# One multiply per turn, half-query waits and a third bank in a four-layer attention kernel with its own planner

## The chip, the cores and the metric

The kernel runs on one core of one Trainium2 chip. The metric is device time in microseconds (us) of one execution. The core has a matrix engine (PE, with its weight load as a row of its own, PEld), a vector engine (DVE), an activation engine (ACT), a general engine (POOL) and a queue engine (SP) that issues nearly all the DMAs here. Matrix results land in PSUM, eight banks of 512 float columns by 128 partitions.

## The reference

The input is a sequence of 2048 rows of width 1024, 32 heads of 32. Four residual layers follow each other, A, B, A, B, with the same weights in both rounds:

```
x = x + A(layernorm(x));  x = x + B(layernorm(x))      # twice
A: q, k, v = x @ wqkv; pq = q @ w_phi; pk = k @ w_phi       # per head
   phi(p) = [softmax(p), softmax(-p)]
   kv = phi(pk)^T v;  z = sum over rows of phi(pk)
   o = (phi(pq) kv) / (phi(pq) z + 1e-6);  A = o @ wo
B: p = softmax(q k^T / sqrt(32));  B = (p v) @ wo           # full attention
```

A is linear in the sequence length. B computes 32 x 2048 x 2048 exponentials in each round, 134 million; they are most of the work of ACT.

## The kernel before, in words

The activations stay transposed in on-chip memory (features on partitions, 2048 rows on the free axis), in four chunks of 512 rows. "Layer" in the code is one round A plus B.

*A.* `layernorm` normalises a chunk; `a_keys` projects keys and values, and adds up kv and z. `a_queries` (line 823) projects a half of the heads of a chunk in four PSUM tiles of class "mm" (class names below), takes two exponentials of each on ACT (line 834), and multiplies by kv (872) and z; `a_out` (898) projects the result in tiles of class "mm" and adds it to x. Each chunk then gets its second layernorm, its keys and values of head group 0 (`b_k`, `b_v`), and chunk 0 its first query (`b_q`).

*B.* Attention goes in turns. A turn is a chunk of 512 queries and a group of four heads: 32 turns a layer, 64 units each. A unit is 128 keys of one head by the 512 queries, one PSUM bank. `group` (1097) takes the next three units, on three different row tiles j of the array, and puts them in one set of three banks: one score group on PE (line 1082), then one exponential on ACT over three banks (1139). Two such sets alternate, so the next score group can be written while ACT works. Some units go to DVE instead (`spare`, `convert`, `exp_dve`): DVE takes a score out of PSUM (1221), and when it has two, computes the exponential by a polynomial (1046, 1048, 1051). When a third unit of a group is lent to DVE, ACT's instruction is two banks wide. A unit may be lent only if everything it needs is done, and DVE looks 36 to 44 units ahead. The exponentials go into the product with v and into the row of ones that gives the denominators (1264); both gather in bank 6.

*A query* has two copies. `b_q` (937) evacuates the projection to copy 0 (DVE, line 943), and `q_swap` writes copy 1 with upper and lower half of the partitions exchanged, by two DMAs (948, 949). Queries of later chunks of the first layers are projected early, sent to DRAM by `q_away` (959) and fetched by `q_back` (three DMAs). A unit with head pair pp and row tile j reads copy (pp + j // 2) mod 2, and of it only the partitions 32j to 32j + 31. `needs` (1076) lists what a unit waits for: the keys, and all three steps of the query.

*End of a turn.* Two half-turns (pp = 0, 1) leave two tiles T, each copied from PSUM by DVE (1279): T[0] has its outputs in partitions 0 to 63 and its denominators in 64 to 127, T[1] the other way round. Four small DMAs (1309) gather the denominators, DVE takes reciprocals (1314), one DMA writes them to DRAM (1315), one reads them back spread over all partitions (1317), and two DVE multiplies of 64 partitions each (1320) make the turn's normalised output oT. The last turn of each layer has a path of its own. The output projection (`b_o`, `b_last`) follows as filler.

*The order.* No line of the code fixes it. Every operation is recorded with an engine, a duration, what it depends on, the buffers it holds and a priority; a planner (`Sched`) runs at build time, starts on each engine the ready operation of the lowest priority number whose buffers can be had, and the instructions are issued in that order. Priorities are times in the planner's units; a turn is 10 of them. `QUOTA` limits the live buffers of a class, among them PSUM classes: "mm" and "fil" had 2. "fil" is the class of filler projections; in attention they have bank 7 alone, before it any bank. Where PE would have nothing to do, the planner puts in matrix passes that compute nothing needed (line 1490 and passes on `onesD`). Engines and the SP queue work strictly in the order issued, PE's weight loads apart. So a change of a quota, of a dependence or of a priority can move any instruction behind it.

Of the kernel before, what the change touches and what calls it, by code (L numbers as in the profile page):

```python
# [10 lines left out]
ACT = mybir.ActivationFunctionType  # L11
ALU = mybir.AluOpType
# [8 lines left out]
C512 = 512  # L21
# [27 lines left out]
class Sched:  # L49
# [133 lines left out]
    def run(self):  # L183
# [27 lines left out]
        while left:  # L211
# [118 lines left out]
EXP2_B, EXP2_C, EXP2_R = -0.9409531310034907, 6.912204565299476, 0.8383392207797716  # L330
LAG = 5
AHEAD_AT = 5
P0 = (133, 163, 246)
# [3 lines left out]
AWAY = (2, 8)  # L337
# [13 lines left out]
def dve_us(n):  # L351
    return n / 960 + 0.15
# [6 lines left out]
def kernel(  # L359
# [11 lines left out]
    nc = tc.nc  # L371
# [85 lines left out]
    op = sch.op  # L457
# [600 lines left out]
    def attention(base, kT, vT, q_of, gate, most, mix, turns, pos):  # L1058
# [17 lines left out]
        def needs(u):  # L1076
            return flat([kT[u[1]][2][u[3] // 2], q_of[(u[0], u[1])][2]])

# [164 lines left out]
        if True:  # L1243
            for qc, g in turns:
# [41 lines left out]
                if end:  # L1286
# [32 lines left out]
                o_b, o_v = sb("oT", C512)  # L1319
                s = [op("DVE", dve_us(512), lambda a=a, k=k, o_v=o_v, r_v=r_v, T=T: nc.vector.tensor_tensor(  # L1320
                    out=o_v()[a, :], in0=T[k][1]()[a, :], in1=r_v()[a, :], op=ALU.mult),
                    [bk], [o_b, r_b, T[k][0]], prio)
                    for k, a in enumerate((lo_, hi_))]
                oTs[qc][g] = (o_b, o_v, s)
# [26 lines left out]
    for layer in range(2):  # L1351
# [18 lines left out]
        for c in chunks:  # L1370
            xnA[c] = layernorm(c, base + 10 * c - 9 if base + c else -16.0, ANY, n=4 if layer else 2)
            a_keys(c, base + 10 * c, wk_s, wv_s, kv, ANY)
# [23 lines left out]
        for c in range(NC):  # L1396
            pr = second + 20 * c
            o_b, o_v = sb("oc", G, C512)
            oc = (o_b, o_v, {})
            for hf in range(2):  # L1400
                a_queries(c, hf, pr + 5 * hf, wq_s, state, oc)
            a_out(c, pr + 22, wo_s, oc)
            xnB[c] = layernorm(c, pr + 23, ANY)
            b_k(0, c, pr + 42, wk0, kT, ANY, "ACT")
            if c == 0:
                q_of[(0, 0)] = b_q(0, 0, pr + 42.5, wq0, ANY)
            for t in range(TB):
                b_v(0, c, t, pr + 43 + 0.1 * t, bv_s[0], vT, ANY, "ACT", (0,) if last else (0, 1))
        gate = []
        at = second + 130  # L1410

        for g in range(1, G):
            pr = at + 10 * pos[(0, g)] - (30 if last else 19)
            w = slab("w2", pr - 1, B_w[:, :, D + g * P:D + (g + 1) * P], P)
            for c in range(NC):
                b_k(g, c, pr + (6 if last else 4) * c, w, kT, FIL, "DVE")
        for c in range(NC):
            for t in range(TB):
                b_v(1, c, t, at + (7 if last else 4.5) * (4 * c + t) + 2, bv_s[1], vT, FIL, "DVE")
                if last:  # L1420
                    b_v(0, c, t, at + 3 * (4 * c + t) + 3, bv_s[0], vT, FIL, "DVE", (1,))
        for g in range(G):
            pr = at + 10 * pos[(0, g)]
            w = slab("w2", pr - 11, B_w[:, :, g * P:(g + 1) * P], P) if g else wq0
            for qc in range(NC):
                if qc < side:
                    if qc or g:
                        pq = at + 10 * pos[(qc, g)]
                        wq = w if pq < pr + 30 else slab("w2", pq - 11, B_w[:, :, g * P:(g + 1) * P], P)
                        q_of[(qc, g)] = b_q(g, qc, pq - 8, wq, FIL)  # L1430
                else:
                    away = q_away(g, qc, pr + (22 if last else AWAY[qc - 2]), w, FIL)
                    q_of[(qc, g)] = q_back(g, qc, at + 10 * pos[(qc, g)] - 12, away)
        oTs = attention(at, kT, vT, q_of, gate, MOST[layer], MIX[layer], turns, pos)
        if last:
            bo_s = [slab("bo", at + 290 + fc, B_o[:, :, fc * C512:(fc + 1) * C512], C512) for fc in range(2)]
        for qc, p0, gap in ((0, P0[0], GAPS[0]), (1, P0[1], GAPS[1]), (2, P0[2], GAPS[2])):
            if last:
                gap = 3.2
                p0 = (226, 252, 278)[qc]  # L1440
# [13 lines left out]
        for i in range(G):  # L1454
            pr = p0 - 7 + 2 * i
            if last:
# [69 lines left out]
```

## Time and profile before

| | us |
|---|---|
| median of 3 runs | 2403.58 (2401.06 to 2406.6) |
| the profiled execution | 2402.28 |
| its span, first to last instruction | 2400.5 |
| PE busy in the span | 2248.0 |
| ACT busy | 2042.4 |
| DVE busy | 1861.2 |
| mean share of the DMA queue of SP | 17.1% of 16 engines |

In the rows that follow, times are from the start of the span. A group row gives line, engine and operation, what it writes and reads, shape, count; then its busy time and the mean of one in ns; then the idle time of the engine ahead of it and what ended it. A mean counts an instruction from its start to its end, and neighbours overlap, so busy times are less than count times mean. Timeline rows give start, length, and in brackets the idle time before. Matrix passes are pipelined and their ends are modelled: a busy PE is not a PE at its peak.

### The profile page before, as it was taken

The numbers are of one execution on the slowest core, as the hardware profiler recorded it, in microseconds if no ns is written. First come the engines' busy times: TensorE is split into PE (matmuls) and PEld (weight loads), VectorE is DVE, ScalarE is ACT, GpSimd is POOL, SyncE is SP. The second block draws the span as 40 slices with busy tenths as digits, with TensorE's granted clock in tenths as the row PEclk, the third lists the DMA queues.
The fourth block names the chain that finished last, engine by engine and source line by source line (L and its number), as shares of the span: only waits on it lengthen the run. The fifth ranks groups of instructions, "written<-read, shape, count | busy, mean of one in ns | idle before, by whom it ended". The sixth has DMA issues, their size and how long they took to land.

```text
span 2400.5 us, 61762 instructions
## 1 busy us (share of the span) xinstructions
PE 2248.0 (94%) x26839; PEld 864.3 (36%) x26904; DVE 1861.2 (78%) x2540; ACT 2042.4 (85%) x1893; POOL 28.0 (1%) x72
## 2 busy tenths in 40 slices
PE   7999999999999998999998999899999999999998
PEld 4443443333333333333333444333333333333333
DVE  6997763565668788987996776456699999998997
ACT  6325657999999999999997456499999999999998
POOL 0000000000000000000000000000000000000000
PEclk9999999999999999999999999899999999999999
DMA  9020010112222221113314100000111111021110
GB/s 220 14 75 1 5 36 17 41 37 48 51 59 73 82 59 55 54 48 110 117 36 143 36 5 25 18 24 26 37 30 41 33 31 33 25 61 42 42 31 28
DMA packets 205192, 117.03 MB, mean 49 GB/s; under 512 B 125304, under 2 KB 194936, under 8 KB 204152
## 3 DMA queue, kind: packets, MB, share of 16 engines
q1 hardware_dynamic: 203864, 110.98, 17.1%
q8 instruction: 210, 3.44, 0.6%
q10 hardware_dynamic: 1056, 2.10, 0.3%
q14 instruction: 62, 0.51, 0.1%
HBM read 77.40 MB, written 15.19 MB: 39 GB/s over the span
## 4 chain that ended last, share of the span: by engine, by line
ACT 35%; PE 13%; issue 9%; DVE 4%; DMA 1%; ACTq 0%; SPq 0%; DVEq 0%
ACT arena L1139 33%; PE psum L503 6%; PE psum L507 2%; PE psum L1082 2%; PE psum L1264 1%; DVE arena L598 1%; ACT arena L696 1%; DVE arena L594 0%; DMA arena<-rd 0%; PE psum L872 0%; DMA arena<-arena 0%; DVE arena L700 0%; PE psum L817 0%; DVE work L1046 0%; DVE arena L709 0%
## 5 line engine op out<-in xcount | busy, mean ns | idle before, releaser
L1139 ACT ACTIVATE arena<-psum 128x1536 bf16<-128x1536 f32 (+1 forms) x1338 | 1712.4, 1553 | 43.0 <-PE psum L1082 38.6
L1264 PE MATMUL psum<-arena 128*32 128x512 bf16 x4096 | 621.1, 383 | 1.5 <-DVE arena L1279 1.4
L1264 PE MATMUL psum<-arena,ones_bf 128*32 128x512 bf16 x4096 | 621.3, 383 | 0.0
L507 PE MATMUL psum<-arena 128*32 128x512 bf16 (+1 forms) x8768 | 607.4, 377 | 12.4 <-DVE xT L1001 2.9
L1082 PE MATMUL psum<-arena 32*128 32x512 bf16 x4096 | 526.5, 383 | 79.2 <-ACT arena L1139 72.7
L503 PE MATMUL psum<-arena 128*128 128x512 bf16 (+1 forms) x1976 | 457.8, 377 | 24.6 <-DVE arena L598 6.0
L1082 PEld LDWEIGHTS <-arena 32*128 32x128 bf16 x4096 | 178.1, 91 | 605.0 <-issue 594.3
L1046 DVE SCALAR_TENSOR_TENSOR work<-work 128x1024 f32<-128x1024 f32 (+1 forms) x310 | 369.4, 1191 | 6.0
L507 PEld LDWEIGHTS <-arena 128*32 128x32 bf16 x8768 | 195.7, 95 | 258.3 <-issue 153.3
L503 PEld LDWEIGHTS <-arena 128*128 128x128 bf16 x2032 | 194.0, 99 | 259.2 <-issue 54.8
L1221 DVE TENSOR_SCALAR work<-psum 128x512 int32<-128x512 f32 x302 | 207.6, 687 | 93.9 <-PE psum L1082 91.2
L1264 PEld LDWEIGHTS <-arena 128*32 128x32 bf16 x4096 | 169.9, 95 | 210.4 <-issue 149.0
L1046 DVE SCALAR_TENSOR_TENSOR arena<-work 128x1024 bf16<-128x1024 f32 (+1 forms) x155 | 184.5, 1190 | 2.6
L1264 PEld LDWEIGHTS <-ones_bf 128*32 128x32 bf16 x4096 | 168.5, 95 | 29.1 <-issue 3.6
L931 DVE CAST arena<-psum 128x512 bf16<-128x512 f32 (+1 forms) x128 | 83.6, 653 | 110.4 <-PE psum L507 110.2
L696 ACT ACTIVATE arena<-psum 128x512 bf16<-128x512 f32 x80 | 42.8, 599 | 85.2 <-PE psum L503 53.8
L1051 DVE TENSOR_SCALAR work<-work 128x1024 int32<-128x1024 int32 (+1 forms) x155 | 104.7, 676 | 3.9
L1048 DVE TENSOR_SCALAR work<-work 128x1024 int32<-128x1024 int32 (+1 forms) x155 | 104.3, 673 | 3.6
L834 ACT ACTIVATE arena<-psum 128x512 bf16<-128x512 f32 x128 | 69.8, 597 | 40.9 <-PE psum L503 32.4
L594 DVE TENSOR_TENSOR arena<-xT,arena 128x1024 f32<-128x1024 bf16 x64 | 78.0, 1220 | 32.3 <-ACT arena L581 32.2
L1279 DVE COPY arena<-psum 128x512 f32<-128x512 f32 x126 | 86.3, 685 | 14.2 <-PE psum L1264 13.2
L507 PE MATMUL psum<-xT,onesD 128*32 128x512 bf16 x1200 | 91.3, 380 | 1.5 <-DVE arena L931 0.6
(97 smaller groups left out, 1387.6 us busy)
## 6 DMA issues: line engine op xcount, KB each, us to landing
arena<-rd SPq DMA_DIRECT2D x62, 256.0 KB
arena<-in_A_wqkv_dram SPq DMA_DIRECT2D x10, 1024.0 KB
arena<-in_B_wqkv_dram SPq DMA_DIRECT2D x35, 256.0 KB
arena<-arena SPq DMA_DIRECT2D x256, 32.0 KB
arena<-in_B_wo_dram SPq DMA_DIRECT2D x32, 256.0 KB
arena<-wd_k SPq DMA_DIRECT2D x8, 1024.0 KB
arena<-arena SPq DMA_DIRECT2D x80, 64.0 KB
arena<-in_A_wo_dram SPq DMA_DIRECT2D x4, 1024.0 KB
```

Source lines behind the costliest of these rows:

```text
L503: nc.tensor.matmul(out_, lhsT=lhsT, rhs=rhs, start=start, stop=stop, skip_group_check=True)
L507: nc.tensor.matmul(out_[ks, :], lhsT=lhsT[:, ks], rhs=rhs, start=start, stop=stop, tile_position=(0, 32 * k), skip_group_check=True)
L594: s1 = op("DVE", dve_us(1024), lambda pr=pr, w_v=w_v: nc.vector.tensor_tensor(out=w_v(), in0=xT[:, pr, csl(c)], in1=m_v().unsqueeze(1).to_ ...
L931: return soon(op("DVE", dve_us(n), lambda: nc.vector.tensor_copy(out=dst(), in_=src()), [dep], bufs, prio))
L1046: return sch.later("DVE", dve_us(n * 512), lambda: nc.vector.scalar_tensor_tensor(out=out_(), in0=in0(), scalar=scalar, in1=in1(), op0=ALU ...
L1048: m = ts(lambda: nc.vector.tensor_scalar(out=x_v().bitcast(I32), in0=y_v().bitcast(I32), scalar1=0x007FFFFF, scalar2=0x3F800000, op0=ALU.b ...
L1051: a = ts(lambda: nc.vector.tensor_scalar(out=y_v().bitcast(I32), in0=y_v().bitcast(I32), scalar1=0x7F800000, scalar2=None, op0=ALU.bitwise ...
L1082: nc.tensor.matmul(out=out_, lhsT=kT[g][1]()[r, pp, d * P:(d + 1) * P], rhs=q_of[(qc, g)][1]()[r, (pp + j // 2) % 2, :], start=True, stop= ...
L1139: ex = make("ACT", act_us(w * C512), lambda: nc.scalar.activation(out=e_v()[:, 0:w * C512], in_=s_v()[:, 0:w * C512], func=ACT.Exp, scale= ...
L1221: pair["got"].append(sch.later("DVE", dve_us(512), lambda: nc.vector.tensor_scalar(out=y_v().bitcast(I32)[:, k, :], in0=s_v(), scalar1=EXP ...
L1264: nc.tensor.matmul(out=a_v()[col:col + 32, :], lhsT=v_v()[:, kc % 4, o:o + DH] if what == 0 else ones_bf[:], rhs=ev()[:, x * C512:(x + 1) ...
L1279: cp = op("DVE", dve_us(512), lambda t_v=t_v, a_v=a_v: nc.vector.tensor_copy(out=t_v(), in_=a_v()), [last], [a_b, t_b], prio - 4)
```

## The change

Four edits, and a set of literals that became names with the values they had.

1. `QUOTA`: "mm" and "fil" from 2 to 3.
2. `needs`: a unit waits only for the step that wrote the partitions it reads: the evacuation for copy 0, one of the two swap DMAs for copy 1.
3. End of a turn: a DMA moves the upper half of T[1] over the upper half of T[0], whose denominators have been read by then; one DVE multiply of 128 partitions makes oT. The move depends on the reciprocals and on the copy of T[1].
4. `QL`: in the second layer the queries are projected at priority 15 ahead of their turn, before 8, and their weight slabs are fetched at 18 ahead, before 11. In the first layer both stay.

```
-QUOTA = {"pk": 3, "pv": 2, "kv": 1, "ln": 2, "mm": 2, "cmp": 2, "bc": 4, "num": 1, "wt": 4, "fil": 2,
+QUOTA = {"pk": 3, "pv": 2, "kv": 1, "ln": 2, "mm": 3, "cmp": 2, "bc": 4, "num": 1, "wt": 4, "fil": 3,
...
+QL = (8, 15)
...
         def needs(u):
-            return flat([kT[u[1]][2][u[3] // 2], q_of[(u[0], u[1])][2]])
+            qc, g, pp, d, j = u
+            q = q_of[(qc, g)][2]
+            return flat([kT[g][2][d // 2], q[(1 if j > 1 else 2) if (pp + j // 2) % 2 else 0]])
...
                 o_b, o_v = sb("oT", C512)
-                s = [op("DVE", dve_us(512), lambda a=a, k=k, o_v=o_v, r_v=r_v, T=T: nc.vector.tensor_tensor(
-                    out=o_v()[a, :], in0=T[k][1]()[a, :], in1=r_v()[a, :], op=ALU.mult),
-                    [bk], [o_b, r_b, T[k][0]], prio)
-                    for k, a in enumerate((lo_, hi_))]
+                mv = dma(prio, lambda T=T: nc.sync.dma_start(out=T[0][1]()[hi_, :], in_=T[1][1]()[hi_, :]),
+                         [rc, T[1][2]], [T[0][0], T[1][0]], kb=128)
+                s = [op("DVE", dve_us(512), lambda o_v=o_v, r_v=r_v, T=T: nc.vector.tensor_tensor(
+                    out=o_v(), in0=T[0][1](), in1=r_v(), op=ALU.mult),
+                    [bk, mv], [o_b, r_b, T[0][0]], prio)]
...
-            w = slab("w2", pr - 11, B_w[:, :, g * P:(g + 1) * P], P) if g else wq0
+            w = slab("w2", pr - (QL[layer] + 3), B_w[:, :, g * P:(g + 1) * P], P) if g else wq0
...
-                        wq = w if pq < pr + 30 else slab("w2", pq - 11, B_w[:, :, g * P:(g + 1) * P], P)
-                        q_of[(qc, g)] = b_q(g, qc, pq - 8, wq, FIL)
+                        wq = w if pq < pr + 30 else slab("w2", pq - (QL[layer] + 3), B_w[:, :, g * P:(g + 1) * P], P)
+                        q_of[(qc, g)] = b_q(g, qc, pq - QL[layer], wq, FIL)
...
```

More of the change, by code (lines that the diff above doesn't have):

```diff
@@ L331 @@
 LAG = 5
+KL = (19, 30)
+KS = (4, 6)
+VS = (4.5, 7)
+VH = 3
+QL = (8, 15)
+AW = 22
+OUT_AT = (226, 252, 278)
+GO = 3.2
+BO = 290
+PT = 2
+QB = 12
+PH = (5, 22, 42)
+LA = 9
 AHEAD_AT = 5
@@ L1370 @@
         for c in chunks:
-            xnA[c] = layernorm(c, base + 10 * c - 9 if base + c else -16.0, ANY, n=4 if layer else 2)
+            xnA[c] = layernorm(c, base + 10 * c - LA if base + c else -16.0, ANY, n=4 if layer else 2)
             a_keys(c, base + 10 * c, wk_s, wv_s, kv, ANY)
@@ L1400 @@
             for hf in range(2):
[L1401 to L1404, printed above, removed]
+                a_queries(c, hf, pr + PH[0] * hf, wq_s, state, oc)
+            a_out(c, pr + PH[1], wo_s, oc)
+            xnB[c] = layernorm(c, pr + PH[1] + 1, ANY)
+            b_k(0, c, pr + PH[2], wk0, kT, ANY, "ACT")
             if c == 0:
-                q_of[(0, 0)] = b_q(0, 0, pr + 42.5, wq0, ANY)
+                q_of[(0, 0)] = b_q(0, 0, pr + PH[2] + 0.5, wq0, ANY)
             for t in range(TB):
-                b_v(0, c, t, pr + 43 + 0.1 * t, bv_s[0], vT, ANY, "ACT", (0,) if last else (0, 1))
+                b_v(0, c, t, pr + PH[2] + 1 + 0.1 * t, bv_s[0], vT, ANY, "ACT", (0,) if last else (0, 1))
         gate = []
@@ L1454 @@
         for i in range(G):
-            pr = p0 - 7 + 2 * i
+            pr = p0 - 7 + PT * i
             if last:
```

17 lines of the change are left out of this document (8 added, 9 removed).

## The prediction

> **What bounds the kernel now.** I read the span by stages first, then the activation engine's groups, then its idle times one by one, then the vector engine and the DMA queue around them. The stages are my cuts: up to 200 us the first layer's key side, to 390 its query side, to 1300 its attention (with the second layer's first keys inside), to 1558 the second layer's linear part, to 2389 its attention, and a tail.
>
> ```profile
> 0.00:200.00 200.00, 176.03 (x1097) 91.27 (x1118) 171.11 (x280) 85.75 (x133) 12.85 (x39) 0.99 0.39 93
> 200.00:390.00 190.00, 181.74 (x991) 74.89 (x1007) 120.18 (x167) 107.82 (x166) 0.00 (x0) 1.00 0.06 15
> 390.00:1300.00 910.00, 855.61 (x11842) 305.88 (x11844) 683.03 (x919) 883.26 (x723) 12.55 (x25) 0.99 0.23 64
> 1300.00:1558.00 258.00, 239.29 (x1359) 106.17 (x1376) 171.95 (x250) 134.32 (x216) 2.59 (x8) 0.97 0.10 33
> 1558.00:2389.00 831.00, 788.76 (x11510) 283.47 (x11507) 708.41 (x915) 829.88 (x654) 0.00 (x0) 1.00 0.12 34
> 2389.00:2400.50 11.50, 6.61 (x63) 2.62 (x57) 6.53 (x10) 1.33 (x3) 0.00 (x0) 1.00 0.27 91
> ```
>
> Columns are stretch, length, then busy time of PE, weight load, DVE, ACT and POOL, granted clock, DMA share and GB/s. In the second attention ACT works 829.88 of 831 us: what leaves ACT there leaves the time. In the first it works 883.26 of 910, so 26.7 us are stalls. The two linear parts are TensorE's. The times of the activation engine that carry the sum:
>
> ```profile
> L1139 ACT ACTIVATE arena<-psum 128x1536 bf16<-128x1536 f32 x1119 | 1569.1, 1621 | 40.2 <-PE psum L1082 36.7 <-PE psum L1264 3.0 <-DVE arena L931 0.4
> L1139 ACT ACTIVATE arena<-psum 128x1024 bf16<-128x1024 f32 x218 | 262.9, 1206 | 2.8 <-PE psum L1082 1.9 <-PE psum L1264 0.9
> L1139 ACT ACTIVATE arena<-psum 128x1536 bf16<-128x1536 f32 x540 | 760.8, 1655 | 2.3 <-PE psum L1082 1.9 <-DVE arena L931 0.4
> L1139 ACT ACTIVATE arena<-psum 128x1024 bf16<-128x1024 f32 x113 | 140.4, 1243 | 0.0
> ```
>
> The first two rows are the whole run, the last two the second attention. One 512-column block more costs 1621 - 1206 = 415 ns in the one, 1655 - 1243 = 412 ns in the other. The 654 instructions of the second attention (540 of three blocks, 113 of two, one of one) filled 829.88 us; with 0.412 per block that leaves about 0.105 us for an instruction itself, so three blocks go through every 1.34 us.
>
> **Part 1: blocks that leave ACT.** The planner decides at build time which blocks of scores DVE exponentiates (L1221 and the rows behind it) and how wide ACT's instructions are. The order of the built instructions of both kernels says what it decided:
>
> ```
>                      ACT instructions of 3 / 2 / 1 blocks     blocks on DVE
> first attention      571/105/0, changed 571/104/0             125, changed 127
> second attention     548/113/1, changed 531/132/0             177, changed 191
> ```
>
> First attention: 2 blocks and one instruction fewer, 2 x 0.412 + 0.105 = 0.9 us. Second: 14 blocks fewer and one instruction more, 14 x 0.412 - 0.105 = 5.7 us. Where the extra blocks lie: by groups of fifty exponentials, 11 of the 14 are in the first 175 of the second attention, which is what the earlier queries (QL 8 to 15) and the narrower `needs` should do, since a block is only lent to DVE when its query is complete. DVE has room there:
>
> ```profile
> 1558.00:1720.00 162.00, 159.34 (x2490) 61.74 (x2486) 93.26 (x141) 161.34 (x126) 0.00 (x0) 1.00 0.10 26
> 1800.00:2360.00 560.00, 523.96 (x7493) 184.63 (x7494) 525.27 (x658) 559.95 (x443) 0.00 (x0) 1.00 0.13 37
> L1221 DVE TENSOR_SCALAR work<-psum 128x512 int32<-128x512 f32 x140 | 96.2, 687 | 17.4 <-PE psum L1082 15.8
> L1046 DVE SCALAR_TENSOR_TENSOR work<-work 128x1024 f32<-128x1024 f32 x140 | 170.7, 1219 | 2.6
> L1046 DVE SCALAR_TENSOR_TENSOR arena<-work 128x1024 bf16<-128x1024 f32 x70 | 85.2, 1217 | 1.2
> L1048 DVE TENSOR_SCALAR work<-work 128x1024 int32<-128x1024 int32 x70 | 48.2, 689 | 1.8
> L1051 DVE TENSOR_SCALAR work<-work 128x1024 int32<-128x1024 int32 x70 | 48.1, 688 | 1.7
> ```
>
> A pair of blocks costs DVE 2 x 0.687 + 0.689 + 0.688 + 2 x 1.219 + 1.217 = 6.4 us, 3.2 us a block. Eleven blocks are 35 us, and DVE is idle for 68.7 us in the first 162 us alone; that idle time is the cover, and where it were gone DVE's copies out of PSUM would be late next. From 1800 on DVE is busy 525.27 of 560 and the block count hardly changes (143 after 142 for 450 exponentials). So the whole 5.7 + 0.9 = 6.6 us counts. Bounds: 0, if late copies hand it all back, and 16 x 0.415 = 6.6.
>
> **Part 2: scores that wait for half a query.** Three of the first attention's stalls look alike.
>
> ```profile
> 440.39 96.16 ACT L1139 ACTIVATE arena<-psum 128x1536 bf16<-128x1536 f32 x75 [2.98 <-PE psum L1082]
> 554.02 54.39 ACT L1139 ACTIVATE arena<-psum 128x1536 bf16<-128x1536 f32 x42 [3.59 <-PE psum L1082]
> 800.31 7.74 ACT L1139 ACTIVATE arena<-psum 128x1536 bf16<-128x1536 f32 x6 [3.40 <-PE psum L1082]
> 929.10 2.79 ACT L1139 ACTIVATE arena<-psum 128x1536 bf16<-128x1536 f32 x2 [3.01 <-PE psum L1264]
> 1111.51 1.45 ACT L1139 ACTIVATE arena<-psum 128x1536 bf16<-128x1536 f32 x1 [1.96 <-PE psum L1082]
> ...
> 549.21 0.69 DVE L943 TENSOR_SCALAR arena<-psum 128x512 bf16<-128x512 f32 x1 [5.11 <-PE psum L507]
> 549.93 0.50 SPq L948 DMA_DIRECT2D arena<-arena  x1
> 550.06 1.90 PE L507 MATMUL psum<-arena 128*32 128x512 bf16 x32
> 550.48 0.60 SPq L949 DMA_DIRECT2D arena<-arena  x1
> 553.53 0.61 PE L1082 MATMUL psum<-arena 32*128 32x512 bf16 x6
> ```
>
> At 549.21 DVE writes a query (L943), SP swaps its halves (L948, L949), and the next scores stand on PE at 553.53, 3.6 us after the query was written. Meanwhile PE does other projections, which the planner put there because it holds the scores until both swaps are home. In the built order such a hole is a run of PE work between two score groups. At 0.217 us for a pass of 512 columns (eight passes in the 1.90 us of the row at 550.06, the last one's drain apart) the three holes of before are 4.33, 4.33 and 4.77 us, each right behind an L943, and made 2.98, 3.59 and 3.40 us of ACT idle: 10.0 us together. In the changed order the first and the third are gone (nothing over 1.75 us stands there), the second is 3.47, and a new place has 2.60 and 2.17 in succession. From the three, a hole costs its length less 1.15 us on average. So 3.47 gives 2.3. The pair, 4.77 in two steps, spends one more exponential of 1.34 against one more score group of 0.32, so 4.77 - 1.15 - 1.0 = 2.6. Left 4.9 us, gained 5.1. Bounds: nothing, if ACT starves elsewhere by as much, and 10.0, if the new holes are covered. The stalls at 929.10 and 1111.51 have other causes (a slow clock, DVE behind a DMA), and nothing in the change aims at them: unchanged, with 0 to 5 us either way in the bounds. A query that is projected earlier only moves its own eight passes, its evacuation, two swaps and a 256 KB slab forward past other fillers; the totals stay, and the q2 quota of three holds them.
>
> **Part 3: one multiply per turn.** Each of 62 turns loses one DVE multiply and gains a DMA on SP's queue, between the write-out of the reciprocals (L1315) and their broadcast (L1317).
>
> ```profile
> L1320 DVE TENSOR_TENSOR arena<-arena 64x512 bf16<-64x512 f32 x124 | 84.7, 683 | 10.3 <-DMA arena<-rd 7.9 <-DMA qd<-arena 0.9
> L894 DVE TENSOR_TENSOR arena<-arena,psum 128x512 bf16<-128x512 f32 x64 | 39.7, 681 | 1.0 <-PE psum L817 0.9
> 532.91 0.33 SPq L1315 DMA_DIRECT2D rd<-arena  x1
> 534.37 0.59 SPq L1317 DMA_DIRECT2D arena<-rd  x1
> 540.23 1.41 DVE L1320 TENSOR_TENSOR arena<-arena 64x512 bf16<-64x512 f32 x2 [0.63 <-DMA qd<-arena]
> ```
>
> A multiply over 128 partitions takes 681 ns (L894) as over 64 it takes 683 (L1320), so DVE is spared 62 x 0.68 = 42 us. None of it is on ACT's chain; it pays for about 13 of the 16 extra blocks at 3.2 us, and is counted there, so here it is 0. On SP the move's issue (0.5 to 0.6 us, as L948 and L949) falls into the 1.13 us between the end of L1315 and the start of L1317, in which SP waits for L1315 to land. It waits for nothing that L1315 had not waited for; queued behind it stand the broadcast and then query swaps and key moves. The broadcast takes until about 540.2, 5.3 us from the end of its issue, so the move is home first. I take 0; the bounds are 10.3 us less DVE wait in all (the idle before L1320, which cannot shrink by more) and 1.5 us more in each turn, if the move shares its engines with the broadcast and delays it by its half of the broadcast's bytes (128 of 256 KB, at the 3 us or so that lie above a swap's 2.5). DVE, which works in order, has (560 - 525.27) / 22 turns (44 multiplies) = 1.6 us idle a turn plus the 0.68 it saves.
>
> The Trainium skill (DMA: Bandwidth & Descriptors, Anatomy of one DMA) gives a DMA a fixed cost of about 2.0 us plus its bytes over 436 GB/s. For the moved 128 KB an estimate by that is 2.3 us, all of it beside the broadcast; if it stood bare, 62 of them would be 143 us of latency, though of DVE's, not ACT's. The swap rows above, home within 2.5 us of the end of issue, agree.
>
> **Part 4: a third bank.** "mm" and "fil" may hold three banks where the linear parts project queries and outputs.
>
> ```profile
> L503 PE MATMUL psum<-arena 128*128 128x512 bf16 x627 | 152.2, 386 | 8.7 <-DVE arena L598 4.4 <-DVE arena L894 2.1 <-ACT arena L834 1.1
> L503 PE MATMUL psum<-arena 128*128 128x256 bf16 x128 | 20.7, 307 | 1.1 <-ACT arena L930 0.9 <-ACT arena L876 0.2
> L872 PE MATMUL psum<-arena 128*128 128x512 bf16 x62 | 18.6, 378 | 3.6 <-ACT arena L876 3.5
> 1480.00:1558.00 78.00, 68.69 (x413) 30.00 (x416) 40.44 (x50) 38.17 (x51) 0.00 (x0) 0.91 0.06 15
> 920.00:940.00 20.00, 17.76 (x220) 5.62 (x216) 13.41 (x17) 16.35 (x15) 0.32 (x1) 0.83 0.05 15
> ```
>
> In 1320 to 1558 the waits that free a bank (ACT's L834, L930) are 2.0 us; the others (L598, L894, L876) are chains through a layer norm or a quotient that no bank shortens. The order starts to differ here, with a projection pulled ahead of a chain, so the bank is used. I take 2 us for both linear parts. Bounds: 1480 to 1558 ran at clock 0.91, so 78 x 0.09 = 7 us more may go with the gaps that brought the low clock, and as much may come back from new gaps: -9 to +7.
>
> The Trainium skill (TensorE: Matmul & The Clock Gate, The HAM clock gate) says an idle window of about 3.4 us halves the clock and a busy one restores it, window by window, at places that drift. The trace agrees in kind (0.91 above); by that rule a reordered stage can gain or lose whole windows, 1.7 us of work each, whatever the sum says.
>
> **Sum.** 6.6 + 5.1 + 0 + 2 = 13.7 us less than the profiled execution. That took 2402.28 us (span 2400.5), 1.3 under the median of 2403.58; so 2388.6, or 2389.9 beside the median: I say 2390. The tail (2389 to 2400.5) is untouched. PE's filler passes fall by 32 in the built order; they stand where PE has nothing to do and count for nothing.
>
> **Rivals.**
> - *Only the blocks count.* Holes are filled with other waits and the bank does nothing: 2403.6 - 6.6 = 2397. For it: half of ACT's idle rows in the first attention have causes the change does not touch. Against: two of three holes are visibly gone. 0.13.
> - *The gaps go too.* All three holes covered (10.0), the low clock of 1480 to 1558 gone (7.0), 6.6 of blocks: 2403.6 - 23.6 = 2380. For it: pulled-ahead projections fill just such gaps. Against: L598 and L876 chains remain. 0.15.
> - *New slow-clock stretches.* A reordered stage gets two more stalls like the one at 929 (3.01 us, clock 0.83 over 20 us) and 7 us in the linear part, which eats the 13.7: 2403, no change. Also the case that the blocks given to DVE return as late copies. 0.14.
> - *The broadcast is late (slower).* The move delays the broadcast, DVE stands at the one multiply in order, and copies and exponentials behind it starve PE. It decides from 1.6 + 0.68 + 13.7/31 = 2.7 us a turn on; at 3.2 it gives 31 x 0.9 = 28 against 13.7: 2418. For it: 45 of the 62 moves stand directly ahead of the broadcast. Against: the 5.3 us broadcast dwarfs the move, and only 7 of 62 turns waited for it so far. 0.12.
>
> **Numbers.** The forecast itself has 0.46, its own range 2384 to 2397. Faster by over 0.2% (about what a measurement of this kernel can tell from no change) is under 2398.8: the forecast, the first and the second rival, 0.74. Same 0.14, slower 0.12. The range for 8 in 10 leaves out the far ends of the second and the last rival: 2375 to 2406.
>
> **What would show it.** ACT's rows: 1102 wide and 236 narrow exponentials, still saturated in the second attention; its busy time about 6.6 us less. Idle before L1139 (40.2 + 2.8) some 5 us less, with two holes left behind query evacuations. One multiply row of 62 at about 685 ns, idle before it not over 20 us. Clock in the last linear stage 0.91 or better. The prediction is wrong if DVE's idle before the multiply exceeds 60 us, if ACT idles in the second attention, or if the linear part before it grows.

## The result and the profile after

The changed kernel takes 2373.3 us, the median of six runs (2370.13 to 2380.23); the kernel before, in the same comparison, 2400.94 (2399.41 to 2406.6). The ratio is 0.9883, its 95% interval 0.987 to 0.9896: faster by 27.6 us, where 13.7 were forecast and 2375 was the lower end of the range. The profiled execution of the changed kernel took 2370.13 us (span 2368.3), the fastest of its six; its 32.2 us of span under the profiled execution of before is 4.6 more than the medians differ by.

By stage, with the cuts where the changed kernel's own stages end (columns as before: stretch, length, busy PE, weight load, DVE, ACT, POOL, clock, DMA share, GB/s):

```profile
0.00:200.00 200.00, 177.10 (x1098) 92.78 (x1118) 171.10 (x280) 85.74 (x133) 12.79 (x39) 0.99 0.39 93
200.00:390.00 190.00, 183.35 (x974) 74.68 (x993) 119.92 (x166) 107.43 (x166) 0.00 (x0) 0.98 0.06 15
390.00:1285.00 895.00, 849.51 (x11824) 305.12 (x11821) 667.47 (x896) 883.41 (x723) 11.52 (x25) 1.00 0.26 69
1285.00:1528.00 243.00, 230.85 (x1358) 103.56 (x1378) 170.74 (x250) 132.56 (x214) 2.59 (x8) 1.00 0.11 35
1528.00:2357.00 829.00, 786.70 (x11432) 281.60 (x11430) 724.44 (x923) 824.61 (x655) 0.00 (x0) 1.00 0.15 39
2357.00:2368.30 11.30, 5.16 (x46) 1.81 (x36) 6.34 (x10) 1.22 (x2) 0.00 (x0) 0.95 0.27 93
```

The first attention is 15 us shorter (895 for 910) with the same ACT work (883.41 for 883.26): only idle time has gone. The second linear part is 15 us shorter (243 for 258), its clock 1.00 for 0.97. The second attention, where the forecast had most of its gain, gives 2 us (829 for 831), although its ACT work fell by 5.3 us (824.61 for 829.88).

The groups of the changed kernel that answer to those of the prediction (lines lie 13 to 17 further down, so L1139 is now L1154, L1320 is L1337):

```profile
L1154 ACT ACTIVATE arena<-psum 128x1536 bf16<-128x1536 f32 x1102 | 1550.1, 1614 | 22.3 <-PE psum L1097 20.3 <-PE psum L1279 1.3
L1154 ACT ACTIVATE arena<-psum 128x1024 bf16<-128x1024 f32 x236 | 282.7, 1198 | 2.4 <-PE psum L1279 2.1 <-PE psum L520 0.3
L1337 DVE TENSOR_TENSOR arena<-arena 128x512 bf16<-128x512 f32 x62 | 42.4, 684 | 8.8 <-DMA arena<-rd 6.2 <-DMA arena<-arena 2.5
```

Idle time of ACT ahead of exponentials fell from 43.0 to 24.7 us. The 62 multiplies of 128 partitions take 684 ns each, and DVE waits 8.8 us in all for them, 10.3 before. The stalls that are left, from the timeline of ACT in the changed kernel:

```profile
493.73 1.45 ACT L1154 ACTIVATE arena<-psum 128x1536 bf16<-128x1536 f32 x1 [0.92 <-PE psum L1097]
496.29 34.24 ACT L1154 ACTIVATE arena<-psum 128x1536 bf16<-128x1536 f32 x27 [1.12 <-PE psum L1097]
...
552.84 7.74 ACT L1154 ACTIVATE arena<-psum 128x1536 bf16<-128x1536 f32 x6 [1.78 <-PE psum L1097]
...
563.04 53.30 ACT L1154 ACTIVATE arena<-psum 128x1536 bf16<-128x1536 f32 x41 [1.06 <-PE psum L1097]
...
1934.96 1.02 ACT L1154 ACTIVATE arena<-psum 128x1024 bf16<-128x1024 f32 x1 [1.70 <-PE psum L1279]
1936.80 1.45 ACT L1154 ACTIVATE arena<-psum 128x1536 bf16<-128x1536 f32 x1 [0.81 <-PE psum L1097]
```

The rows at 493, 496 and 552 are the query holes that the built order had shown: 0.92 + 1.12 + 1.78 = 3.8 us. The row at 563 is another kind of stall. DVE stood for 5.26 us at the reciprocals of a turn, until a DMA landed; PE waited 0.78 us for the copy that DVE makes after them, and ACT waited for PE:

```profile
561.20 0.25 DVE L1329 RECIPROCAL arena<-arena 128x16 f32<-128x16 f32 x1 [5.26 <-DMA arena<-arena]
562.05 0.61 PE L520 MATMUL psum<-arena 128*32 128x512 bf16 x8 [0.78 <-DVE arena L944]
```

Apart from these little is left in the first attention (single gaps of under 0.9 us), where before there were stalls near 808, 929, 1111, 1172 and 1293 as well. In the second attention ACT idles for 4.1 us, which the prediction had named as a sign that it is wrong.

For the experiments one table serves. "First attention" runs from the start of ACT's unbroken work to the last exponential of the first layer; "linear part" from there to the unbroken work of the second layer; "second attention" to the last exponential. Idle is ACT's, from its timeline. All lengths are of the one profiled execution of each kernel, ratios of the timed runs against the kernel before on the same chip.

```
                          ratio   95% interval      first att. (idle)   linear   second att. (idle)
before                                              909.1 (25.2)        257.4    830.6 (0.6)
changed                   0.9883  0.987  - 0.9896   891.4 ( 8.4)        243.4    828.7 (4.1)
mm 3 alone                0.9944  0.9922 - 0.9966   907.5 (23.8)        244.1    831.7 (1.2)
needs alone               1.0004  0.999  - 1.0018   904.5 (20.2)        256.2    830.9 (1.2)
merge alone               1.0000  0.9988 - 1.0011   903.0 (19.5)        257.9    832.4 (5.1)
QL alone                  0.9983  0.997  - 0.9996   904.1 (20.3)        257.1    827.3 (0.5)
changed without banks     0.9988  0.9976 - 1.0001   911.0 (27.1)        257.2    826.4 (1.6)
changed without needs     0.9931  0.9916 - 0.9946   907.3 (23.6)        248.6    825.2 (1.0)
changed without merge     0.9916  0.99   - 0.9932   905.0 (22.4)        243.9    827.0 (0.8)
changed without QL        0.9891  0.9876 - 0.9906   893.7 ( 9.8)        245.7    832.2 (4.7)
changed, two multiplies   0.9899  0.9882 - 0.9916   894.5 ( 9.5)        244.5    831.4 (6.1)
changed, v shifted        0.9954  0.9939 - 0.9969   902.8 (19.3)        253.8    828.6 (3.6)
changed, k shifted        0.9987  0.9973 - 1.0001   919.4 (35.2)        246.3    825.0 (0.9)
changed, away shifted     0.9949  0.9931 - 0.9966   913.2 (29.6)        246.9    825.2 (0.9)
mm 4 alone                0.9948  0.9931 - 0.9964   907.0 (21.0)        246.9    831.3 (1.1)
fil 3 alone               0.9962  0.9949 - 0.9975   902.5 (18.5)        249.8    830.5 (0.7)
before, k shifted         1.0015  1.0004 - 1.0027   913.1 (29.5)        257.5    830.9 (0.6)
before, away shifted      1.0006  0.9997 - 1.0016   907.6 (23.4)        257.2    831.2 (1.0)
```

Two orders appear more than once: "QL alone" has the order of before up to the second attention, "changed without QL" and "two multiplies" have that of the changed kernel. So 909.1 and 904.1 are one order in two executions, and 891.4, 893.7 and 894.5 are another: one order repeats within about 5 us in these five executions.

### The profile page after: what moved, and what is told of

It is laid out like the page before. It is cut to its first block, busy times and chain, and to the rows that moved or that the text cites. A ratio compares the mean times of both kernels' runs of the same rounds, so it can differ in the third digit from the quotient of the medians.

```text
span 2368.3 us, 61633 instructions
## 1 busy us (share of the span) xinstructions
PE 2232.7 (94%) x26710; PEld 859.6 (36%) x26776; DVE 1860.0 (79%) x2524; ACT 2035.0 (86%) x1893; POOL 26.9 (1%) x72
## 4 chain that ended last, share of the span: by engine, by line
ACT 44%; PE 33%; issue 11%; DVE 9%; SPq 2%; DMA 2%; ACTq 0%; DVEq 0%
ACT arena L1154 41%; PE psum L516 14%; PE psum L520 7%; PE psum L1279 5%; PE psum L1097 5%; DVE arena L713 1%; SPq L551 1%; ACT arena L709 1%; PE psum L885 1%; DVE work L1059 1%; DVE arena L722 1%; DMA arena<-arena 1%; DVE arena L761 1%; DVE arena L607 1%; ACT arena L572 1%
## 5 line engine op out<-in xcount | busy, mean ns | idle before, releaser
L1154 ACT ACTIVATE arena<-psum 128x1536 bf16<-128x1536 f32 (+1 forms) x1338 | 1706.1, 1541 | 24.7 <-PE psum L1097 20.3
L516 PE MATMUL psum<-arena 128*128 128x512 bf16 (+1 forms) x1979 | 451.9, 374 | 17.0 <-DVE arena L1315 3.7
L1059 DVE SCALAR_TENSOR_TENSOR work<-work 128x1024 f32<-128x1024 f32 (+1 forms) x322 | 387.9, 1205 | 6.2
L1236 DVE TENSOR_SCALAR work<-psum 128x512 int32<-128x512 f32 x318 | 218.2, 687 | 98.9 <-PE psum L1097 94.4
L1059 DVE SCALAR_TENSOR_TENSOR arena<-work 128x1024 bf16<-128x1024 f32 (+1 forms) x161 | 193.7, 1203 | 2.1
L1064 DVE TENSOR_SCALAR work<-work 128x1024 int32<-128x1024 int32 (+1 forms) x161 | 109.9, 683 | 4.1
L1061 DVE TENSOR_SCALAR work<-work 128x1024 int32<-128x1024 int32 (+1 forms) x161 | 109.5, 680 | 3.7
L1294 DVE COPY arena<-psum 128x512 f32<-128x512 f32 x126 | 86.1, 683 | 20.1 <-PE psum L1279 17.4
```

Source lines behind the costliest of these rows:

```text
L516: nc.tensor.matmul(out_, lhsT=lhsT, rhs=rhs, start=start, stop=stop, skip_group_check=True)
L1059: return sch.later("DVE", dve_us(n * 512), lambda: nc.vector.scalar_tensor_tensor(out=out_(), in0=in0(), scalar=scalar, in1=in1(), op0=ALU ...
L1061: m = ts(lambda: nc.vector.tensor_scalar(out=x_v().bitcast(I32), in0=y_v().bitcast(I32), scalar1=0x007FFFFF, scalar2=0x3F800000, op0=ALU.b ...
L1064: a = ts(lambda: nc.vector.tensor_scalar(out=y_v().bitcast(I32), in0=y_v().bitcast(I32), scalar1=0x7F800000, scalar2=None, op0=ALU.bitwise ...
L1154: ex = make("ACT", act_us(w * C512), lambda: nc.scalar.activation(out=e_v()[:, 0:w * C512], in_=s_v()[:, 0:w * C512], func=ACT.Exp, scale= ...
L1236: pair["got"].append(sch.later("DVE", dve_us(512), lambda: nc.vector.tensor_scalar(out=y_v().bitcast(I32)[:, k, :], in0=s_v(), scalar1=EXP ...
```

## Experiments: each edit alone

```
 QUOTA of before: "mm": 2 -> 3
```

> The kernel before with only the quota of class mm at 3. Theory 1 (each gain belongs to one edit): the third projection bank alone shortens the second layer's linear part, from the last exponential of the first attention to the point from which ACT is busy without a break, from 258 us to about 243, half of it time at the low clock; in the first attention the query holes stay (two runs of 4.55 and 4.77 us of PE work between score groups); whole kernel 12 to 20 us less, about 2385. Theory 2 (reordering alone moves it, by where stalls and low-clock windows happen to fall): linear part anywhere in 243 to 260, whole kernel between 2385 and 2405, no tie to the bank.

Measured 2387.32 us (ratio 0.9944) and a linear part of 244.1 us. Theory 1 holds for the linear part; theory 2 allowed the same length, and falls only with the later kernels, in which the length goes with the bank. TensorE's groups in the linear part of this kernel (idle before them at the end of each row), then the whole part:

```profile
L503 PE MATMUL psum<-arena 128*128 128x512 bf16 x696 | 162.3, 379 | 5.3 <-ACT arena L834 1.8 <-DVE arena L1300 1.8 <-DVE arena L894 1.2
L872 PE MATMUL psum<-arena 128*128 128x512 bf16 x64 | 19.0, 379 | 1.7 <-ACT arena L876 1.6
...
1298.70:1542.80 244.10, 232.83 (x1368) 103.49 (x1367) 170.42 (x249) 132.38 (x215) 2.58 (x8) 1.00 0.11 36
```

and the same in the kernel before:

```profile
L503 PE MATMUL psum<-arena 128*128 128x512 bf16 x674 | 164.2, 385 | 11.8 <-DVE arena L598 4.4 <-DVE arena L894 2.1 <-ACT arena L834 1.9
...
1301.00:1558.50 257.50, 238.79 (x1349) 105.77 (x1365) 171.59 (x250) 133.34 (x216) 2.59 (x8) 0.97 0.10 33
```

Two things shrank: waits of the projections (11.8 to 5.3 us, and the layer norm's L598, 4.4 us, is no longer among the releasers), and PE's busy time for the same work (238.79 to 232.83), which is the clock, 0.97 against 1.00.

```
 needs() of before: only the query's own half, as in the diff
```

> The kernel before with only the narrower wait of the scores. Theory 1: the holes of 4.33, 4.33 and 4.77 us become 2.38, 3.68 + 1.95 and 2.17 + 2.17, so the first attention loses about 5 us of ACT idle, the linear part stays at 258, the second attention too: about 2396. Theory 2: the stalls that no edit aims at (3 us near 929, 2 + 1 us near 1111 in the profile of before) move as well, so the first attention ends anywhere from 15 us less to 5 us more.

2399.57 us, no change that can be measured, where theory 1 had 2396. The holes in the order are smaller, as read; the idle time behind them is hardly less (timelines of ACT and, in the last two rows, PE in this kernel, two lines further down than before):

```profile
439.59 108.68 ACT L1141 ACTIVATE arena<-psum 128x1536 bf16<-128x1536 f32 x84 [1.07 <-PE psum L1084]
550.26 1.45 ACT L1141 ACTIVATE arena<-psum 128x1536 bf16<-128x1536 f32 x1 [2.00 <-PE psum L1084]
554.04 61.60 ACT L1141 ACTIVATE arena<-psum 128x1536 bf16<-128x1536 f32 x48 [2.33 <-PE psum L1084]
...
796.15 1.45 ACT L1141 ACTIVATE arena<-psum 128x1536 bf16<-128x1536 f32 x1 [0.88 <-PE psum L1084]
800.61 10.00 ACT L1141 ACTIVATE arena<-psum 128x1536 bf16<-128x1536 f32 x8 [3.00 <-PE psum L1084]
...
553.55 0.61 PE L1084 MATMUL psum<-arena 32*128 32x512 bf16 x5 [1.05 <-DMA arena<-arena]
800.11 0.61 PE L1084 MATMUL psum<-arena 32*128 32x512 bf16 x6 [1.33 <-DMA arena<-arena]
```

1.07 + 2.00 + 2.33 + 0.88 + 3.00 = 9.3 us, against 10.0 of one-piece holes before. Only the hole that stayed in one piece got cheaper (1.07 for 2.98). The two that were split did not: 3.68 + 1.95 of PE work cost 4.3 us where 4.33 in one piece cost 3.6, and 2.17 + 2.17 cost 3.9 where 4.77 cost 3.4. The last two rows show why the second pieces are dear: PE had run out of other work and stood 1.05 and 1.33 us at the scores until a DMA landed, here that of a swap, for which half of the units still wait.

```
 end of a turn of before: move by DMA, one multiply, as in the diff
```

> The kernel before with only the move by DMA and the single multiply. Theory 1: DVE has 42 us less to do; 7 more blocks leave ACT in the second attention (2.9 us), but two new runs of 3.0 and 3.5 us of PE work stand there between score groups (2 us each); query holes of the first attention stay; linear part stays: 2399 to 2402. If the DVE time itself is what removed the stalls near 929 and 1111, the first attention loses 5 us more: 2395. The third view, that the move delays the broadcast: idle of DVE before the multiply over 60 us, and slower than before.

2398.96 us, ratio 1.0000. As theory 1 had it. The second attention has 4.5 us more of idle (5.1 against 0.6), most of it in two stalls, which eats the 2.9 us of blocks. The first attention took 903.0 us, 1 to 6 less than the two executions of the order of before, so theory 2 is not excluded by the stage; the whole kernel shows nothing of it. DVE's idle before the multiply is 4.5 us in all, so in this order the broadcast is not late:

```profile
1652.61 27.46 ACT L1139 ACTIVATE arena<-psum 128x1536 bf16<-128x1536 f32 x21 [1.62 <-PE psum L1082]
...
1709.19 22.15 ACT L1139 ACTIVATE arena<-psum 128x1536 bf16<-128x1536 f32 x18 [1.83 <-PE psum L1082]
...
L1322 DVE TENSOR_TENSOR arena<-arena 128x512 bf16<-128x512 f32 x62 | 42.5, 685 | 4.5 <-DMA arena<-rd 3.5 <-DMA arena<-arena 0.7 <-DMA qd<-arena 0.2
```

```
 second layer of before: b_q at pq - 15, its slab at 18 ahead
```

> The kernel before with only the second layer's queries 15 ahead. The order up to the second attention is that of before, so first attention and linear part stay. Theory 1: 9 blocks fewer on ACT, 2 instructions more: 9 x 0.412 - 0.2 = 3.5 us less, 2397. Rival: ACT gets idle time in the second attention, as in the changed kernel (6.4 us against 2.3), which takes the gain back: 2400 to 2402.

2395.63 us, ratio 0.9983: 3.5 to 4 us (the interval runs from 1 to 7), theory 1. The second attention took 827.3 us with 0.5 idle, so here all of the blocks that left ACT left the time.

## Experiments: the changed kernel without each edit

```
 QUOTA: "mm": 3 -> 2, "fil": 3 -> 2
```

> The changed kernel with mm and fil back at 2. Theory 1: it loses what the bank brought: linear part back to about 258 us, whole kernel 12 to 18 us slower than the changed one, about 2388. Theory 2: linear part anywhere from 243 to 260.

2399.64 us: nearly the whole gain is gone, where theory 1 had about 2388. The linear part is back at 257.2, as theory 1 says. But the first attention lost more still, 911.0 for 891.4, and no bank of class mm is used there.

```
 needs(): all three steps of the query, as before
```

> The changed kernel with scores waiting for the whole query again. Theory 1: query holes of 2.38, 2.38, 4.55 and 2.17 us against 2.60 + 2.17 and 3.47: the first attention loses 3 to 6 us, the rest stays: 2377 to 2380. Theory 2: anything from 2372 to 2390, with the difference in stalls that stand behind no query.

2386.33 us, 13 us slower than the changed kernel, where theory 1 allowed 4 to 7, and inside the wide range of theory 2. The first attention is at 907.3. The linear part of 248.6 holds 5.6 us more filler in its built order (228.6 us of passes, 223.0 in the changed kernel), since the planner moved a projection into it.

```
 end of a turn: two multiplies of 64 partitions, no move, as before
```

> The changed kernel with the two multiplies of 64 partitions and no move. Theory 1: holes of 3.03 + 1.95, 3.47 and 4.33 us, so 3 us more idle in the first attention, 3 blocks more on ACT in the second (1.2 us): 2377. If freeing DVE was worth more than blocks, stalls behind DVE come back: 2385 and above.

2381.76 us, 8 us slower, between the two expectations. The first attention is at 905.0 with 22.4 idle, of which the query holes are 7.4; the second is 827.0, shorter than in the changed kernel.

```
 QL = (8, 15) -> (8, 8)
```

> The changed kernel with the second layer's queries 8 ahead. Order the same up to the second attention. Theory 1: 7 blocks more on ACT and 3 instructions fewer in the second attention, 7 x 0.412 - 0.3 = 2.6 us, and a hole of 3.25 us: 2376 to 2378. Rival: ACT idle in the second attention falls back from 6.4 to 2.3 us and it is as fast, 2372 to 2374.

2376.26 us, 3 us slower, as theory 1 had it, though the intervals of the two ratios overlap; the second attention takes 832.2 us, 3.5 more. The whole table says it more surely. With the earlier queries the second attention took 825 to 829 us in eight of nine kernels (831.4 in "two multiplies"), without them 830.5 to 832.4 in all nine.

Banks, needs and merge are each worth 8 to 26 us taken away, while of these three alone only the bank is worth anything. The excess is in the first attention, which is at 891 to 895 us with all three and at 903 to 911 with any one missing. Either they work only together, or the changed kernel's order is a lucky one.

## Experiments: joint effect or lucky order

```
 the one multiply issued as two of 64 partitions, at the same place of the order
```

> The changed kernel, its order and the move by DMA kept, but the normalising multiply is issued as two of 64 partitions each, so DVE has its 42 us back at the same places. Theory A (the merge matters through DVE's time): the ACT idle of the first attention that no query explains (15 us before, 3.5 in the changed kernel) comes back in part: 5 to 10 us slower than the changed kernel, 2379 to 2383. Theory B (the merge matters only through the order the planner makes with it): within 3 us of the changed kernel, 2371 to 2376.

2375.67 us, theory B. Half of the 42 us lies in the first attention: DVE works 688.10 us there, where the changed kernel has 667.47 (the row of the changed kernel stands at the end of this section).

```profile
393.70:1288.20 894.50, 848.88 (x11795) 301.03 (x11792) 688.10 (x927) 883.67 (x721) 11.50 (x25) 1.00 0.26 69
```

These 20.6 us more of DVE work at the same order changed the first attention by 3.1 us, within the spread of an order, and the whole kernel by less than its intervals tell apart. So DVE's time is not what the merge brings.

```
 VS = (4.5, 7) -> (4.6, 7)
```

> The changed kernel with the first layer's later values 4.6 units apart for 4.5: a shift that means nothing by itself and reorders the first attention. All four edits kept. If the edits together cure the first attention, it takes 890 to 896 us again. If the 892 us was a lucky order, it takes 900 to 911 like the six kernels that lack one edit or have one alone. Linear part 243 to 246 by either.

2388.75 us. First attention 902.8: lucky order. The linear part of 253.8 missed both: its order holds 7.4 us more filler (230.3 us of passes for 223.0).

```
 KL = (19, 30) -> (19.3, 30)
```

> The same with the first layer's keys 19.3 units ahead for 19. Joint cure: first attention 890 to 896 us. Lucky order: 900 to 911. Linear part 243 to 246 by either.

2395.99 us. First attention 919.4, the longest of all, with all four edits in place and query holes of 3.8 us that equal the changed kernel's; the linear part, 246.3, is a little over its range. Its largest stalls stand elsewhere, and the clock is low around them:

```profile
908.31 1.45 ACT L1154 ACTIVATE arena<-psum 128x1536 bf16<-128x1536 f32 x1 [2.79 <-DVE arena L1337]
1121.42 1.45 ACT L1154 ACTIVATE arena<-psum 128x1536 bf16<-128x1536 f32 x1 [5.84 <-PE psum L1097]
1217.92 3.01 ACT L1154 ACTIVATE arena<-psum 128x1536 bf16<-128x1536 f32 x2 [3.70 <-PE psum L1097]
...
900.00:940.00 40.00, 34.76 (x448) 12.91 (x446) 32.76 (x49) 35.19 (x31) 0.65 (x2) 0.91 0.17 52
1110.00:1150.00 40.00, 33.12 (x433) 10.29 (x425) 26.93 (x36) 31.52 (x26) 0.00 (x0) 0.87 0.33 87
...
DVE arena L1337 <- DMA arena<-rd: 17.4, 7, 7.5
...
1118.61 0.69 DVE L1337 TENSOR_TENSOR arena<-arena 128x512 bf16<-128x512 f32 x1 [7.46 <-DMA arena<-rd]
1120.15 0.59 PE L1279 MATMUL psum<-arena 128*32 128x512 bf16 x1 [6.10 <-DVE arena L1294]
```

The row with three numbers at its end is from the view of who waited for whom: DVE waited 17.4 us in seven turns, 7.5 at the longest, for the broadcast of a turn. The last two rows are that longest wait. DVE stood at the multiply for 7.46 us, PE waited 6.10 us for the copy that DVE makes behind it, and ACT idled 5.84 us (the row at 1121). So the slower rival of the prediction does occur, in single turns. Whether this order places the multiply early or the broadcast late is not shown.

```
 AWAY = (2, 8) -> (2.3, 8.3)
```

> The same with the first layer's queries that go out to DRAM at 2.3 and 8.3 units for 2 and 8. One query hole more (3.03 + 1.95 us). Joint cure: first attention 892 to 899 us. Lucky order: 902 to 912. Linear part 243 to 246 by either.

2387.94 us, first attention 913.2, just beyond the range of the lucky order; linear part 246.9, just over its own. Lucky order again. ACT's work in the first attention hardly differs between these kernels, only the idle time does. The first attention as one stretch, for the kernel with k shifted:

```profile
392.20:1311.60 919.40, 852.74 (x11763) 303.39 (x11760) 673.27 (x903) 883.23 (x721) 10.71 (x25) 0.99 0.25 68
```

and for the changed kernel:

```profile
393.40:1284.70 891.30, 845.86 (x11795) 303.81 (x11792) 667.47 (x896) 882.19 (x721) 11.52 (x25) 1.00 0.26 70
```

## Experiments: the bank, and orders of the kernel before

```
 QUOTA of before: "mm": 2 -> 4
```

> The kernel before with mm at 4. If a free bank is what the second linear part lacked, the third covers it and the fourth adds little: linear part 242 to 246. If the gain was a matter of order and low-clock windows, it lies anywhere from 243 to 258. First attention 900 to 912 by the spread of orders so far.

2387.05 us, linear part 246.9, just over the expected 242 to 246: the fourth bank adds nothing over the third.

```
 QUOTA of before: "fil": 2 -> 3
```

> The kernel before with only fil at 3. By the PE work that stands in the linear part (189.2 + 12.13 + 21.44, as before) and the banks of the queries untouched: linear part 255 to 259. If fil shares in the gain: under 252. First attention 900 to 915.

2390.85 us, ratio 0.9962, and a linear part of 249.8: fil does share in this one order, against the first expectation. Its waits are close to those of before, its clock is not:

```profile
L503 PE MATMUL psum<-arena 128*128 128x512 bf16 x696 | 162.7, 379 | 9.5 <-DVE arena L598 4.4 <-DVE arena L894 2.3 <-DVE arena L1300 1.7
L872 PE MATMUL psum<-arena 128*128 128x512 bf16 x64 | 19.0, 378 | 4.1 <-ACT arena L876 3.2 <-DVE arena L862 0.8
...
1295.10:1544.90 249.80, 233.41 (x1376) 103.61 (x1375) 170.90 (x250) 133.00 (x216) 2.59 (x8) 1.00 0.11 34
```

This splits the 14 us of the linear part. PE's busy time fell by 5.4 us (238.79 to 233.41) at full clock, and the waits by about 2; a third mm bank keeps the clock as well and takes another 5 us of waits (244.10 - 232.83 = 11.3 us in which PE is not busy, for 16.4 with fil and 18.7 before).

```
 before: keys of the first layer 19 -> 19.3 units ahead
```

> The kernel before with the first layer's keys 19.3 units ahead for 19, nothing else. Lucky order of the changed kernel: first attention 900 to 915, like all other orders, total 2395 to 2408. If the changed kernel's edits are what makes 892 possible, this says the same; only a value under 897 would say that such luck is as likely without the edits.

2402.29 us, first attention 913.1.

```
 before: AWAY = (2, 8) -> (2.3, 8.3)
```

> The kernel before with the first layer's queries that go out to DRAM at 2.3 and 8.3 units for 2 and 8, nothing else. Holes behind queries are larger here (4.33, 5.63, 4.55 us). First attention 903 to 918, linear part 256 to 259, total 2398 to 2412.

2401.66 us, first attention 907.6, linear part 257.2. Both as expected. With them, fourteen different orders of the first attention, with and without the edits, took 902 to 919 us, and one, the changed kernel's, 891 to 895.

## Why the prediction was right and wrong

**Blocks that leave ACT: right in size, and nearly lost again.** ACT's work fell by 5.3 us in the second attention, 5.7 forecast. The earlier queries alone deliver 3.3 us of it as time. In the changed kernel the second attention is only 1.9 us shorter (828.7 for 830.6), since its idle time rose from 0.6 to 4.1 us, most of it near 1935; so one sign of being wrong came true, in a stage that cost little. Six other orders with the same edit had 0.5 to 1.6 idle, one 3.6.

**Half a query: the number came near, the reason did not hold.** Query holes cost 3.8 us after 10.0; 4.9 were worked out from the built order. But the narrower wait alone gives 9.3, since it splits two of three holes. That holes vanished in the changed kernel belongs to its order as a whole, so that the term came near is luck. The rule of 1.15 us less than the length does not carry over to split holes.

**Stalls said to be unchanged: the first failed step.** The term "unchanged, with 0 to 5 us either way" was sized by the two stalls near 929 and 1111. The idle time behind no query fell from 15.2 to 4.6 us, 10.6 us, and the prediction had set its change at nothing. That an edit does not aim at a stall was no reason: the edits reorder everything, and the term follows the order. The shifted orders show that the four edits together do not make the gain: with all four in place the same term went from 4.6 up to about 31.

**One multiply: right.** The move is home in time in all but two of 62 turns (2.5 us of the 8.8 that DVE waited are put to a DMA between tiles, the rest to the broadcast), DVE's 42 us are worth nothing that these runs can tell (two multiplies: within the spread), and the bounds held. The slower rival has its place, the multiply in DVE's order, but only in single turns. The fixed cost that the prediction quotes from the Trainium skill (DMA: Bandwidth & Descriptors, Anatomy of one DMA) stands in that section for DMAs that the general engine issues. SP issues this one; no run times the move alone, and the sum did not use it.

**A third bank: the second failed step.** I took 2 us, with -9 as the far end, from the waits that name a bank's releaser. It brought 14. The waits that I had called chains that no bank shortens shrank too (with mm at 3, L598's 4.4 us are no longer listed, and the idle time before L872, mostly L876's, is 1.7 us where it was 3.6): the built order shows a projection pulled ahead at each such place, and after the first scores of the second layer 6.7 us of PE work where 21.0 stood. That the last chunk's chain thereby runs under other chunks' work is argued from this order; mm at 3 against 2 shows the gain, not the path. And the 7 us of low clock that I put into the range belonged into the term: the clock of the linear part is 0.97 in before, and 0.99 or 1.00 in every kernel with the bank. The Trainium skill (TensorE: Matmul & The Clock Gate, The HAM clock gate) says that an idle window of about 3.4 us halves the clock, and that these windows run freely. The trace agrees on the half and on the length, 0.50 over 3.4 us, and differs on the idling: PE was busy for 45% of the window ahead (both in the last section). That the windows run freely no run here shows. With fil at 3 the waits were nearly those of before and the clock was 1.00, so gaps alone do not settle it.

**The sum.** 14 us of bank, 6 of query holes, 10.6 of other stalls, 1.9 net in the second attention make the 32 us of the profiled executions, small shifts at the start of the first attention apart. The rival "the gaps go too", 2380, was the nearest. The direction was right, the size half, and of the 32 us about 17 came with an order that none of three small shifts kept.

What stays open is which property of the changed kernel's order spares it the stalls from 800 on. Some of these stalls are seen to begin with DVE at an instruction that waits for a DMA of the turn's end (563 in the changed kernel, 1121 with the keys shifted), but no run takes single stalls out of an order.

## What to carry to other kernels

Where a planner orders a kernel, compare an edit only after a few meaningless shifts of its constants: here they moved one stage between 891 and 919 us with every edit in place, more than any edit moved any stage by itself. What repeated over all orders belongs to the edit: the linear part took 243 to 254 us in all ten kernels with a third mm bank or a fourth, and 256 to 258 in all seven with two banks of each class. What appeared in one order belongs to that order. In a stage that TensorE bounds, price its gaps together with the low clock that may follow them, and do not exclude a wait because its releaser is a chain: here such waits shrank with one more free tile.

## What was not expected of the hardware

The spread between runs of one program goes with the clock: the kernel before took 2389.25 us at a mean clock of 0.998 and 2404.05 at 0.991, 15 us, and the changed kernel 2370.13 at 0.997 and 2380.23 at 0.991. Which of the two causes the other, stalls or low clock, these runs do not tell apart. Gaps of under 2 us each, several in a row (1.42, 0.46, 0.89 and 1.17 us in the twelve us from 1505 of the kernel before), went with a clock of 0.73 over 1506 to 1524; no gap there was as long as 3 us.

```profile
1506.07 0.81 PE L503 MATMUL psum<-arena 128*128 128x512 bf16 x4 [1.42 <-DVE arena L598]
1507.34 3.37 PE L503 MATMUL psum<-arena 128*128 128x256 bf16 x16 [0.46 <-ACT arena L930]
1513.27 0.59 PE L872 MATMUL psum<-arena 128*128 128x512 bf16 x2 [0.89 <-ACT arena L876]
1516.30 0.59 PE L872 MATMUL psum<-arena 128*128 128x512 bf16 x2 [1.17 <-ACT arena L876]
...
1506.00:1524.00 18.00, 14.34 (x70) 5.73 (x71) 9.32 (x16) 9.09 (x15) 0.00 (x0) 0.73 0.10 23
1504.20:1507.60 3.40, 1.52 (x11) 0.82 (x9) 2.39 (x3) 0.90 (x2) 0.00 (x0) 1.00 0.00 0
1507.60:1511.00 3.40, 3.40 (x20) 2.00 (x17) 1.18 (x2) 1.11 (x4) 0.00 (x0) 0.50 0.16 36
```

The clock is half over 1507.6 to 1511.0, and in the 3.4 us ahead of it PE was busy for 1.52 us, 45%: it was not idle. A stretch like that is not enough either. In the kernel with only fil at 3 PE was busy for 1.35 of 3.4 us at about the same place, and the clock stayed full:

```profile
1506.10:1509.50 3.40, 1.35 (x9) 0.46 (x8) 1.95 (x4) 1.95 (x4) 0.00 (x0) 1.00 0.00 0
1509.50:1513.00 3.50, 3.07 (x17) 0.95 (x16) 2.48 (x5) 1.73 (x2) 0.00 (x0) 1.00 0.33 75
```

In all five timed runs of that kernel the mean clock was 0.996 to 0.998. Windows with places of their own, in which the same gaps count or not by where they fall, would fit both; these traces do not settle it.
